# First keys and queries loaded by halves of the heads on 128 partitions, transposed 128 rows at a time

## The chip, the core and the metric

The kernel runs on one core of a Trainium2 chip. A core has five engines that run beside each other and meet through semaphores: TensorE (PE; its weight loads are listed apart, as PEld), VectorE (DVE), ScalarE (ACT), GpSimd (POOL) and SyncE (SP). TensorE reads from the on-chip memory SBUF and writes to the accumulation memory PSUM; VectorE and ScalarE carry results from there back into SBUF. Transfers run on 16 DMA engines. Both memories have 128 partitions. The metric is the device time of one execution in microseconds; the median of several plain runs counts, and a profile is one further execution that the hardware profiler recorded.

## What is computed

The inputs are q, k and v of shape 8 batches x 8 heads x 576 positions x 64, in float32, and two weight matrices, 512 x 2048 and 2048 x 512. Each head runs attention in a window of 32 positions to either side, and the joined heads go through a two-layer network:

```python
scores = (1 / sqrt(64)) * q @ k^T
mask   = abs(pos_i - pos_j) <= 32            # within one batch
attn   = softmax(where(mask, scores, -1e9))
x      = (attn @ v), heads side by side       # 4608 rows x 512
h      = x @ w_in                             # 4608 x 2048
out    = (h * sigmoid(1.702 * h)) @ w_out     # 4608 x 512, float32
```

## The kernel before

The 4608 rows (8 batches of 576) are cut into 36 units of 128 rows, and four units make a tile of 512 rows. For a unit the kernel forms scores of keys against queries per head, with keys on the partitions (`scores`), takes their exponential on ScalarE, multiplies the band mask in on VectorE (`band`), multiplies with the values on TensorE (`values`; a column of ones beside the values gives the sums), divides by them on VectorE (`norm`) and transposes the result (`x_T`, `x_T2`). The tile then goes through the two layers, later ones with Strassen-like sums that save products; tile 0 is done plainly (`layer1_plain`, `layer2_plain`).

The order of all instructions is written out by hand: each engine runs its own in the order in which the program names them, and a wait holds everything behind it on that engine. `run` calls `opening`, which deals with units 0 to 7, and then a steady loop over tiles.

The change lies in `opening`. There SBUF is empty, and TensorE has nothing to do until the first keys have come. What happens, in order:

- POOL issues all loads. Those from float32 inputs to the kernel's 16-bit tiles convert on the way. The order is: first part of the keys (320 rows of all 8 heads), first part of the queries (256 rows), the identity matrix that the transposes need (computed on POOL), values of units 0 to 2, the first quarter of `w_in`, the mask (computed on POOL), second parts of keys and queries (256 rows each), the rest of the mask (`cut_mask`), then further weights and values, and keys and queries of the next tile (`load_four`). From the ninth transfer on, each waits until the one eight places ahead of it has landed.
- `load_first` puts rows onto 64 partitions, j successive rows of a head (j is 5 or 4) on one partition, so that each contiguous piece read is j x 64 numbers. The first parts of keys and queries lie on partitions 0 to 63, the second parts on 64 to 127.
- `T_first` transposes: for each head and each of the j rows one TensorE instruction with 64 rows and 64 columns, into two PSUM banks of four heads each. A bank is copied to SBUF by VectorE or ScalarE, so that head 2 hp lies on partitions 0 to 63 and head 2 hp + 1 on partitions 64 to 127 of slot hp.
- `keep_busy` issues products of zeros into a PSUM bank that nobody reads. There are twenty ahead of the first transposes, six between those of keys and queries, four after them, and more later in the opening.
- `odd_v` copies halves of two value tiles into one on VectorE, so that each copy waits for the loads of two successive units. In VectorE's order the copies for units 0 and 1 stand ahead of the mask products of units 0 and 1, and those for units 2 and 3 ahead of the mask products of units 2 and 3.

All products come from one helper, line 70 of the program; the program's names tell them apart in the profile (`junk` unread, `sc` scores, `pv` values, `h` first layer, `o` second layer, `tp` transposes).

Of the kernel before, what the change touches and what calls it, by code (L numbers as in the profile page):

```python
# [16 lines left out]
BF16 = mybir.dt.bfloat16  # L17
# [9 lines left out]
class _Kernel:  # L27
# [107 lines left out]
    FIRST = {"k": ((0, 320, 5), (320, 256, 4)), "q": ((32, 256, 4), (288, 256, 4))}  # L135

    def load_first(self, c, part):
        if "first" not in self.stage:
            s = self.sb("g", [128, self.H, 9, self.D], BF16, 2, "kq1")
            self.stage["first"] = {"k": s[:, :, 0:5], "q": s[:, :, 5:9]}  # L140
        lo, n, j = self.FIRST[c][part]
        src = {"q": self.q, "k": self.k}[c]
        self.nc.gpsimd.dma_start(self.stage["first"][c][64 * part:64 * part + 64, :, 0:j],
                                 src[0, :, lo:lo + n, :].rearrange("h (p j) d -> p h j d", j=j))

    def kq_tile(self, t):

# [9 lines left out]
    def T_first(self, c, part, tags, engs):  # L157

        lo, n, j = self.FIRST[c][part]
        lo -= 32 * (c == "q")  # L160
        dst = self.kq_tile(0)["kq".index(c)][:, :, lo:lo + n]
        r = slice(64 * part, 64 * part + 64)
        src = self.stage["first"][c][r]
        for i, (tag, eng) in enumerate(zip(tags, engs)):
            tp = self.bank(tag, [128, 2, j, 64], BF16, "tp")
            for h in range(4):
                for x in range(j):
                    self.nc.tensor.transpose(tp[64 * (h % 2):64 * (h % 2) + 64, h // 2, x, :], src[:, 4 * i + h, x, :],  # L168
                                             self.ident[r, r])
            self.copy(eng, dst[:, 2 * i:2 * i + 2, :].rearrange("x h (p j) -> x h p j", j=j),  # L170
                      tp.rearrange("x h j p -> x h p j"))

    def load_four(self, c):

# [387 lines left out]
    def opening(self):  # L562
# [23 lines left out]
        self.load_four("q")  # L586
        self.load_w1(3)
        dve.tensor_copy(self.identh, self.ident)
        self.keep_busy(20, "E")
        self.T_first("k", 0, "AC", (dve, act))  # L590
        self.keep_busy(6, "E")
        self.T_first("q", 0, ("LA", "LB"), (dve, act))
        self.keep_busy(4, "E")
        for u in (5, 6):
            self.load_v(u)
        self.load_w2(0)
# [21 lines left out]
        h, n, gelus = [], [0], []  # L618
# [293 lines left out]
```

## Time and profile before

| what | us |
|---|---|
| median of 3 plain runs | 288.01 (287.84 to 289.57) |
| profiled execution, its own time | 289.7 |
| its span, first to last instruction | 288.0 |
| TensorE busy | 277.7 (96%) |
| VectorE busy | 218.3 (76%) |
| ScalarE busy | 193.9 (67%) |
| POOL busy | 126.9 (44%) |
| first key load, issue to landing | 5.0 |
| first query load, issue to landing | 5.7 |
| TensorE idle in the first 32 us, at most places | 1.3 at the start, 0.6 ahead of the first transposes, 1.4 ahead of the transposes of units 2 and 3 |

A row of a timeline has the start in us, the duration, the engine, the line of the program and the operation, what is written and read with its shape, and the count of successive instructions of this kind; in brackets stands the idle time ahead of it and what ended that. Durations of overlapping instructions are counted once. Matmuls are pipelined: a group's length over its count is the price of one, after a tail for the last one to drain.

### The profile page before, as it was taken

How to read it: one execution, taken by the hardware profiler on the slowest of the kernel's cores; microseconds unless marked ns; L12 is line 12 of the kernel's file. 1: busy time of each engine (PE TensorE's matmuls, PEld its weight loads, DVE VectorE, ACT ScalarE, POOL GpSimd, SP SyncE). 2: the span in 40 equal slices, each digit the busy share in tenths (PEclk: the TensorE clock that was granted, in tenths of full speed). 3: DMA queues.
4: the chain of work that ended last, by engine and by line, in shares of the span. 5: the costliest groups of instructions: out<-in, count | busy, mean ns of one | idle time of the engine just before them, and what ended most of it. 6: DMA issues, size and time to landing. Idle time of an engine off the chain costs nothing.

```text
span 288.0 us, 9119 instructions
## 1 busy us (share of the span) xinstructions
PE 277.7 (96%) x3770; PEld 229.8 (80%) x3770; DVE 218.3 (76%) x502; ACT 193.9 (67%) x340; POOL 126.9 (44%) x192
## 2 busy tenths in 40 slices
PE   7997999999999998999999999999999999999994
PEld 5775856777678887888888888888888888888883
DVE  0676798888877986798879887978788878946731
ACT  2437594789887668676967696689668865568410
POOL 8965457599499954467155917350210000000000
PEclk9999999999999999999999999999999999999999
DMA  8999999999999999999979999998432150301033
GB/s 94 188 193 198 184 204 153 177 99 140 184 134 153 209 132 198 93 180 146 182 106 181 142 177 100 193 116 148 95 77 64 47 112 12 81 2 73 2 110 112
DMA packets 146986, 37.37 MB, mean 130 GB/s; under 512 B 133888, under 2 KB 142592, under 8 KB 146944
## 3 DMA queue, kind: packets, MB, share of 16 engines
q0 software_dynamic: 104464, 18.42, 91.4%
q1 hardware_dynamic: 42032, 17.84, 34.8%
q8 instruction: 29, 0.48, 0.7%
q10 hardware_dynamic: 448, 0.52, 0.6%
q14 instruction: 13, 0.11, 0.1%
HBM read 36.83 MB, written 9.44 MB: 161 GB/s over the span
## 4 chain that ended last, share of the span: by engine, by line
PE 87%; DVE 4%; ACT 3%; issue 2%; DMA 2%; ACTq 0%; POOLq 0%
PE h L70 39%; PE o L70 36%; PE pv L70 3%; PE sc L70 3%; DVE x L294 2%; DMA kq<-in_k_dram 2%; PE junk L70 2%; ACT p L256 1%; PE tp L168 1%; PE tp L322 1%; ACT L256 1%; DVE p L264 1%; PE tp L189 1%; PE tp L232 1%; DVE rec L293 1%
## 5 line engine op out<-in xcount | busy, mean ns | idle before, releaser
L419 ACT ACTIVATE g<-h 128x512 f16<-128x512 f32 x128 | 72.1, 598 | 35.9 <-PE h L70 35.7
L70 PEld LDWEIGHTS <-g 128*128 128x128 f16 x576 | 54.5, 98 | 9.7
L70 PEld LDWEIGHTS <-a 128*128 128x128 f16 x512 | 49.3, 98 | 11.0 <-issue 0.8
L70 PE MATMUL h<-xs,a 128*128 128x256 f16 x384 | 57.6, 272 | 0.1
L70 PE MATMUL o<-w,g 128*128 128x256 f16 (+1 forms) x320 | 55.1, 294 | 0.0
L70 PEld LDWEIGHTS <-w 128*128 128x128 f16 x512 | 49.2, 98 | 7.3 <-issue 0.6
L70 PE MATMUL h<-xT,w 128*128 128x256 f16 x384 | 53.9, 273 | 0.6 <-issue 0.5
L199 POOL DMA_DIRECT2D ve<-in_v_dram x40 | 34.3, 863 | 44.0 <-issue 37.0
L70 PEld LDWEIGHTS <-gs 128*128 128x128 f16 x384 | 36.9, 98 | 6.2 <-issue 1.5
L256 ACT ACTIVATE p<-sc 128x512 bf16<-128x512 f32 x72 | 36.6, 619 | 3.7 <-PE sc L70 3.6
L70 PE MATMUL o<-b,gs 128*128 128x256 f16 x256 | 37.8, 273 | 1.3 <-issue 0.9
L70 PE MATMUL o<-b,g 128*128 128x256 f16 x256 | 37.3, 273 | 0.0
L432 DVE TENSOR_TENSOR h<-h,s 128x512 f32<-128x512 f32 x32 | 22.4, 698 | 18.7 <-PE h L70 18.7
L67 ACT COPY h<-h 128x512 f32<-128x512 f32 x32 | 18.7, 585 | 16.5 <-PE h L70 16.1
L131 POOL DMA_DIRECT2D kst<-in_k_dram x31 | 26.4, 855 | 6.9 <-PE tp L232 3.4
L131 POOL DMA_DIRECT2D qst<-in_q_dram x35 | 28.1, 805 | 2.8 <-DMA w<-in_moe_w_out_dram 2.7
L294 DVE TENSOR_TENSOR x<-pv,rec 128x256 f16<-128x256 f32 (+1 forms) x53 | 27.6, 520 | 1.8
L264 DVE TENSOR_TENSOR p<-p,mask 128x1024 bf16<-128x1024 bf16 x36 | 24.7, 687 | 2.6 <-ACT p L256 2.6
L438 DVE TENSOR_TENSOR h<-h,s 128x512 f32<-128x512 f32 x32 | 22.4, 700 | 4.7 <-PE h L70 4.2
L209 POOL COPY vo<-ve 64x264 int32<-64x264 int32 x28 | 13.1, 467 | 25.8 <-PE pv L70 24.7
L67 ACT COPY s<-h 128x512 f32<-128x512 f32 x32 | 19.1, 598 | 1.5 <-PE h L70 0.2
L70 PE MATMUL h<-xs,w 128*128 128x256 f16 x128 | 19.2, 273 | 0.0
(85 smaller groups left out, 367.9 us busy)
## 6 DMA issues: line engine op xcount, KB each, us to landing
out_dram<-o_sb SPq DMA_DIRECT2D x33, 256.0 KB, 3.0
ve<-in_v_dram POOLq DMA_DIRECT2D x32, 128.0 KB, 5.8
kst<-in_k_dram POOLq DMA_DIRECT2D x25, 128.0 KB, 5.9
qst<-in_q_dram POOLq DMA_DIRECT2D x21, 128.0 KB, 5.7
w<-in_moe_w_in_dram POOLq DMA_DIRECT2D x4, 512.0 KB, 8.7
w<-in_moe_w_out_dram POOLq DMA_DIRECT2D x4, 512.0 KB, 13.5
qst<-in_q_dram POOLq DMA_DIRECT2D x7, 96.0 KB, 5.1
kq<-in_q_dram POOLq DMA_DIRECT2D x2, 256.0 KB, 6.2
```

The lines of the kernel that those rows point to most:

```text
L67: (eng.copy if eng is self.nc.scalar else eng.tensor_copy)(out, in_)
L70: self.nc.tensor.matmul(out, lhsT, rhs, start=start, stop=stop, skip_group_check=True)
L131: self.nc.gpsimd.dma_start(t[off:off + n], src[b, :, s:s + n, :].rearrange("h s d -> s h d"))
L168: self.nc.tensor.transpose(tp[64 * (h % 2):64 * (h % 2) + 64, h // 2, x, :], src[:, 4 * i + h, x, :], self.ident[r, r])
L199: self.nc.gpsimd.dma_start(t[off:off + n, :, :self.D], self.v[b, :, s:s + n, :].rearrange("h s d -> s h d"))
L209: eng.tensor_copy(words(vo[64:128]), words(self.ve[u % 9][64:128]))
L256: self.nc.scalar.activation(p[:, eo].rearrange("k h s -> k (h s)"), sc[eo], AF.Exp, scale=self.scale)
L264: (eng or self.nc.vector).tensor_mul(pv, pv, msk.to_broadcast([128, 8, 2, SQ]))
L294: dve.tensor_mul(x[:, 4 * at:4 * (at + n), :].rearrange("p (b h) d -> p b h d", b=n), acc[:, :, :, :D], r.to_broadcast([128, n, 4, D]))
L419: act.activation(g[:, f, 256 * half:256 * half + 256], bank.rearrange("p (i n) -> p i n", i=2), AF.Gelu_apprx_sigmoid)
L432: dve.tensor_add(e, b, s7)
L438: dve.tensor_add(c, b, s7)
```

## The change

The first parts of keys and queries now use all 128 partitions: heads 0 to 3 lie on partitions 0 to 63, heads 4 to 7 on 64 to 127. Each of the two loads becomes two, one for each half of the heads. A transpose then takes 128 rows (the same rows of two heads, h and h + 4) and gives 64 x 128, so that there are half as many, of twice the columns. A PSUM bank holds heads 0, 1, 4, 5 or 2, 3, 6, 7, and the copy writes every second slot. The second parts are loaded and transposed as before, the keys' now on partitions 0 to 63. Three calls of unread products change: 60 of 96 columns for 20 of 256 in front, and 4 of 128 columns for 6 and for 4 of 256.

```diff
@@ -135,13 +135,21 @@
     FIRST = {"k": ((0, 320, 5), (320, 256, 4)), "q": ((32, 256, 4), (288, 256, 4))}
 
     def load_first(self, c, part):
+
+        D = self.D
         if "first" not in self.stage:
-            s = self.sb("g", [128, self.H, 9, self.D], BF16, 2, "kq1")
-            self.stage["first"] = {"k": s[:, :, 0:5], "q": s[:, :, 5:9]}
+            s = self.sb("g", [128, 68 * D], BF16, 2, "kq1")
+            self.stage["first"] = {("k", 0): s[:, 0:20 * D], ("q", 0): s[:, 20 * D:36 * D],
+                                   ("k", 1): s[0:64, 36 * D:68 * D], ("q", 1): s[64:128, 36 * D:68 * D]}
         lo, n, j = self.FIRST[c][part]
-        src = {"q": self.q, "k": self.k}[c]
-        self.nc.gpsimd.dma_start(self.stage["first"][c][64 * part:64 * part + 64, :, 0:j],
-                                 src[0, :, lo:lo + n, :].rearrange("h (p j) d -> p h j d", j=j))
+        src = {"q": self.q, "k": self.k}[c][0, :, lo:lo + n, :].rearrange("h (p j) d -> p h (j d)", j=j)
+        dst = self.stage["first"][c, part]
+        if part:
+            self.nc.gpsimd.dma_start(dst.rearrange("p (h x) -> p h x", h=8), src)
+            return
+        for g in range(2):
+            self.nc.gpsimd.dma_start(dst[64 * g:64 * g + 64].rearrange("p (h x) -> p h x", h=4),
+                                     src[:, 4 * g:4 * g + 4, :])
 
     def kq_tile(self, t):
 
@@ -159,16 +167,24 @@
         lo, n, j = self.FIRST[c][part]
         lo -= 32 * (c == "q")
         dst = self.kq_tile(0)["kq".index(c)][:, :, lo:lo + n]
-        r = slice(64 * part, 64 * part + 64)
-        src = self.stage["first"][c][r]
+        src = self.stage["first"][c, part].rearrange("p (h j d) -> p h j d", j=j, d=self.D)
+        r = slice(64, 128) if part and c == "q" else slice(0, 64)
         for i, (tag, eng) in enumerate(zip(tags, engs)):
-            tp = self.bank(tag, [128, 2, j, 64], BF16, "tp")
-            for h in range(4):
-                for x in range(j):
-                    self.nc.tensor.transpose(tp[64 * (h % 2):64 * (h % 2) + 64, h // 2, x, :], src[:, 4 * i + h, x, :],
-                                             self.ident[r, r])
-            self.copy(eng, dst[:, 2 * i:2 * i + 2, :].rearrange("x h (p j) -> x h p j", j=j),
-                      tp.rearrange("x h j p -> x h p j"))
+            if part:
+                tp = self.bank(tag, [128, 2, j, 64], BF16, "tp")
+                for h in range(4):
+                    for x in range(j):
+                        self.nc.tensor.transpose(tp[64 * (h % 2):64 * (h % 2) + 64, h // 2, x, :], src[:, 4 * i + h, x, :],
+                                                 self.ident[r, r])
+                self.copy(eng, dst[:, 2 * i:2 * i + 2, :].rearrange("x h (p j) -> x h p j", j=j),
+                          tp.rearrange("x h j p -> x h p j"))
+                continue
+            tp = self.bank(tag, [128, j, 2, 64], BF16, "tp")
+            for x in range(j):
+                for h in range(2):
+                    self.nc.tensor.transpose(tp[64 * h:64 * h + 64, x].rearrange("x g p -> x (g p)"), src[:, 2 * i + h, x, :],
+                                             self.ident)
+            self.copy(eng, dst[:, i:i + 3:2, :].rearrange("x g (p j) -> x g p j", j=j), tp.rearrange("x j g p -> x g p j"))
 
     def load_four(self, c):
 
@@ -586,11 +602,11 @@
         self.load_four("q")
         self.load_w1(3)
         dve.tensor_copy(self.identh, self.ident)
-        self.keep_busy(20, "E")
+        self.keep_busy(60, "E", 96)
         self.T_first("k", 0, "AC", (dve, act))
-        self.keep_busy(6, "E")
+        self.keep_busy(4, "E", 128)
         self.T_first("q", 0, ("LA", "LB"), (dve, act))
-        self.keep_busy(4, "E")
+        self.keep_busy(4, "E", 128)
         for u in (5, 6):
             self.load_v(u)
         self.load_w2(0)
```

## The prediction, made before the result was known

> **What bounds the kernel now.** I read the page first, then the chain of waits over the first 45 us, since the change touches nothing later, and then the engines' timelines there.
>
> ```profile
> span 288.0 us, 9119 instructions
> ...
> 120.00:200.00 80.00, 80.00 (x1100) 69.01 (x1099) 67.10 (x155) 60.27 (x105) 41.05 (x63) 1.00 1.66 151
> ...
> PE o L70 <- issue: 0.9, 1, 0.9
> ```
>
> The second line is a stretch of the table by windows (length, busy time of PE, PEld, DVE, ACT, POOL, granted clock, DMA share, GB/s): from 120 to 200 us TensorE is busy all 80.00 us. The third is the longest of TensorE's five waits between 32 us and the end; none of the five names a DMA. So time won or lost in the opening should arrive at the end.
>
> ```profile
> 1.33 4.97 DMA kq<-in_k_dram
> ...
> 6.34 1.35 PE tp L168 x40
> 7.70 1.40 PE junk L70 x6
> 9.09 1.02 PE tp L168 x32
> 10.11 0.97 PE junk L70 x4
> 11.08 1.00 PE sc L70 x32
> 12.08 2.02 PE junk L70 x10
> ```
>
> This is the chain (start, length, what): the first key load, then TensorE without a gap, and 2.37 us of that (1.40 + 0.97) are products that nobody reads. The chain names the last releaser only, so VectorE and ScalarE have to be read beside it:
>
> ```profile
> 10.21 0.59 ACT L67 COPY kq<-tp 128x512 bf16<-128x512 bf16 x1 [1.79 <-PE tp L168]
> 11.71 2.06 ACT L256 ACTIVATE p<-sc 128x512 bf16<-128x512 f32 x4 [0.91 <-PE sc L70]
> ...
> 11.55 0.58 DVE L210 COPY vo<-ve 64x264 int32<-64x264 int32 x1
> 12.90 0.69 DVE L264 TENSOR_TENSOR p<-p,mask 128x1024 bf16<-128x1024 bf16 x1 [0.77 <-ACT p L256]
> 13.81 0.69 DVE L264 TENSOR_TENSOR p<-p,mask 128x1024 bf16<-128x1024 bf16 x1 [0.22 <-ACT p L256]
> ```
>
> The second mask product ends at 14.50; the second unit's values cannot start before it, whatever the ten unread products do. What counts is therefore: scores, exponentials, mask products.
>
> **The change, part by part.** *The clock.* Equal products take two prices:
>
> ```profile
> 1.27 4.45 PE L70 MATMUL junk<-idle 128*128 128x256 bf16 x20 [1.27 <-DVE spark L567]
> ...
> 14.94 0.83 PE L70 MATMUL junk<-idle 128*128 128x256 bf16 x6
> 15.60 0.39 PE L310 MATMUL tp<-identh,x 128*128 128x128 f16 x4
> ...
> 28.88 1.11 PE L189 MATMUL tp<-ident,o_sb 128*64 128x128 bf16 x32
> ```
>
> At 14.94 six products of 256 columns take 0.83 us: less a tail of some 0.2, 0.107 each. At 1.27 twenty take 4.45: 0.213 each, twice as much, though the granted clock in the windows there reads 1.00. The ten from 12.08 still take 2.02, so the slow price held to about 14 us. The Trainium skill, "TensorE: Matmul & The Clock Gate", Part 1, says that the array runs at half rate until a free-running window of about 3.4 us has been busy; the trace agrees on the factor of two, and its granted-clock column does not show it.
>
> *Sixty products of 96 columns for twenty of 256.* By columns at the slow price: 0.213 x 96/256 = 0.080 each, 4.8 us, so from 1.27 to about 6.1, where the old ones were through at 5.7. The cover is the first key load, which lands at 6.30: nothing is paid. Each product also loads 128 columns of weights. At 15.60 load and product of 128 columns run at (0.39 - 0.22) / 3 = 0.057 apart, so at half rate the load costs at most 0.114, and sixty would take 6.8 us; below, it is hidden. I take hidden, because the 64x64 transposes at 6.34 have a load each and go at 0.03.
>
> *The first transposes.* Keys: 20 instructions of 128 rows for 40 of 64; queries 16 for 32. The form stands at 28.88: (1.11 - 0.22) / 32 = 0.028 fast, so 0.055 slow. Keys cost 20 x 0.055 + 0.22 = 1.3 (was 1.35), queries 1.1 (was 1.02 to 1.09). The streamed columns are the same (20 x 128 = 40 x 64): no gain from the array. At the fast price they would be 0.8 and 0.7. The copies keep their number and sizes, with another order of strides, which no row prices; I take 0, within 0.1 either way.
>
> *Unread products between.* 6 and 4 of 256 become 4 and 4 of 128: 1.40 and 0.97 become 0.43 each slow, 0.23 fast: 0.97 + 0.54 = 1.5 off TensorE's row. What is late next is the query load.
>
> *Loads.* Two transfers become four, all issued by POOL ahead of everything else it does:
>
> ```profile
> 1.33 0.82 POOL L143 DMA_DIRECT2D kq<-in_k_dram  x1 [0.80 <-POOLq L896]
> 2.14 0.69 POOL L143 DMA_DIRECT2D kq<-in_q_dram  x1
> ...
> 3.36 2.67 POOL L199 DMA_DIRECT2D ve<-in_v_dram  x3
> ...
> 9.83 0.56 POOL L111 MEMSET mask<- 64x32 bf16 x4
> ...
> 14.98 0.65 POOL L178 DMA_DIRECT2D o_sb<-in_q_dram  x1
> kq<-in_k_dram POOLq DMA_DIRECT2D x1, 320.0 KB, 5.0
> kq<-in_q_dram POOLq DMA_DIRECT2D x1, 256.0 KB, 5.7
> 3.00:3.50 0.50, 0.50 (x4) 0.38 (x3) 0.06 (x1) 0.00 (x0) 0.42 (x3) 1.00 0.73 42
> 4.50:5.00 0.50, 0.50 (x4) 0.38 (x3) 0.00 (x0) 0.00 (x0) 0.50 (x1) 1.00 1.35 198
> ```
>
> An issue of 32 KB takes 0.65, one of 256 KB 0.69, so two more cost about 1.3 us of POOL. The identity is then ready at 4.7 instead of 3.41, hidden by the load; the mask at 11.7 instead of 10.39; the value loads, the second parts and all weights are issued 1.3 later. Landing: the keys' second half is issued at about 2.05; if the latency of 4.97 held in full, keys land at 7.0. If the engines' rate decides (42 GB/s at 3 us, 198 at 4.5), the bytes are the same and they land at 6.3. I take 6.4, since half the bytes need less of that latency. The first transpose waits for both halves, and all of TensorE's order stands behind it. Queries: landed at 2.14 + 5.7 = 7.84; the last half goes out at 3.4, so 7.84 to 8.4 (3.4 + 4.97); I take 8.1.
>
> One rule speaks against this part: the Trainium skill, "DMA: Bandwidth & Descriptors", Rules for kernel authors, says that two transfers to disjoint partition halves serialize on the same engines and one transfer should be used. No run here shows it yet; it would leave only the issue time, and its result is the second rival.
>
> *Sum with the slow price throughout.* Keys land 6.4, transposed by 7.7, four products to 8.1, queries to 9.2. ScalarE's copy of them ends at 9.8 instead of 10.80: 1.0 gained. The exponentials go to 10.7 to 12.8. The mask product is held by the mask (11.7) and by the copies of values ahead of it in VectorE's order, which were through at 11.55 + 0.58 = 12.1 and will be by 12.1 to 12.4 (below). The second mask product ends at 13.5, so 1.0 is left.
>
> *With the clock open by 6 us.* Queries are the wait: 8.1 + 0.7 + a copy's end, 9.4: 1.4 gained. Exponentials end at 12.3; the bands end between 12.6 and 13.8.
>
> *What takes some back.* VectorE's next group:
>
> ```profile
> 19.78 0.30 DVE L209 COPY vo<-ve 64x264 int32<-64x264 int32 x1
> 20.09 0.29 DVE L210 COPY vo<-ve 64x264 int32<-64x264 int32 x1
> ...
> 21.79 0.69 DVE L264 TENSOR_TENSOR p<-p,mask 128x1024 bf16<-128x1024 bf16 x1 [0.51 <-ACT p L256]
> 22.77 0.69 DVE L264 TENSOR_TENSOR p<-p,mask 128x1024 bf16<-128x1024 bf16 x1 [0.29 <-ACT p L256]
> 11.11 2.27 POOL L199 DMA_DIRECT2D ve<-in_v_dram  x3
> DMA to landing us min/median/max: 5.1/5.2/5.2
> DMA to landing us min/median/max: 7.5/7.8/8.5
> 8.00:9.00 1.00, 1.00 (x6) 0.46 (x3) 0.03 (x1) 0.42 (x1) 0.93 (x3) 1.00 2.37 152
> 10.00:12.00 2.00, 2.00 (x57) 1.37 (x52) 1.91 (x5) 0.87 (x2) 1.91 (x6) 1.00 1.28 209
> ```
>
> The first three value loads land 5.1 to 5.2 us after their issue: the third, issued at about 5.1, at 10.2; now 10.2 to 11.5, and the copies that need it end by 12.4. The next three take 7.5 to 8.5: the fourth, issued at 11.11, lands at 19.6, when its copy at 20.09 is nearly due. The latency grows while the engines move 150 to 210 GB/s: loads queue behind bytes, so a later issue need not land later. Bounds: 0 and the whole 1.3. I take 0.2, nearer to the rows of full engines. Then the copies run from 19.8 to 20.8, and the mask products, which waited for exponentials, end at 22.3 instead of 23.46. The gain of 1.0 to 1.4 passes, trimmed to 1.1 to 1.5. All later transfers are issued when an earlier one has landed (POOL's own waits), so they keep their distance.
>
> Against the profiled execution's own time, 289.7 us (span 288.0 and 1.7 around it): 289.7 - 1.1 = 288.6 with the slow price, 289.7 - 1.5 = 288.2 with the clock open. The median of the plain runs is 288.01, their spread 287.84 to 289.57. The profiled time lies beside the highest. I read the lower two as executions in which the clock opened early: by the same rows the old kernel would then have its queries transposed by 8.5, its bands ended by 12.6 and, held by value copies at 19.65, its second bands by 21.9, 1.5 ahead of the profile, about the 1.7 seen. So the change brings the common execution little: what an open clock gave, the shorter unread products give too, and not twice. **Forecast 288.2 us**, own range 287.5 to 288.8.
>
> **The rivals.** *The profile's offset is constant.* Then 1.7 is a cost of profiling, the plain executions have the slow price, and the gain of 1.1 to 1.5 shows in full: 288.01 - 1.2 = 286.8. For it: the profile is above the median. Against: one plain run reached 289.57. Chance 0.27.
>
> *The split loads take the place of the unread products (slower).* If every transfer lands 1.3 later, the fourth value load lands at 20.9, the copies end at 22.1, the second bands at 23.5: nothing is gained on the profile, 289.6, and the common execution loses 1.5. It decides once that landing moves by more than about 0.4. For it: two more issues ahead of all loads; against: growing latencies at full engines. Chance 0.16.
>
> *Weight loads hold the front.* Sixty at 0.114 end at 8.1; the keys wait 1.7 and 1.5 is given back: about 289.9. Chance 0.04, by the 0.03 above.
>
> *The change does not do what it says:* the clock stays shut as before in every execution. That is the sum with the slow price, 288.6, inside the forecast's own range. Forecast with this, 0.49. The rest, 0.04, is for a larger gain, should full partitions speed the transfers.
>
> **How the numbers follow.** A difference of under 1% (2.9 us) is about what a measurement of this kernel cannot tell from no change. All cases lie inside it. Faster by more needs 1.4 us beyond the best case: 0.03; slower by more needs both slow rivals: 0.04; so 0.93 remains. The range takes the constant offset with 0.2 beyond it, 286.6, and most of the slower rival, 289.4.
>
> **What would show it.** In the new profile: a front of sixty that ends between 5 and 6.3; keys transposed from 6.3 to 6.6 and queries from 8 to 8.4; POOL's mask finished near 11.7; the fourth value load landing between 19.6 and 20.0; the second unit's bands ending before 13.7. An own time of the new profile near 288.4, close to its median, speaks for my reading of the offset; one 1.7 above its median for the constant. I am wrong if keys land after 7, or if value copies after 20.3 hold the bands.

## The result, and the profile after

The changed kernel takes 292.20 us (median of 4 runs, 291.54 to 292.70) against 288.59 (4 runs, 287.84 to 289.57): a ratio of 1.0109, 95% interval 1.0076 to 1.0142, some 3.1 us slower by the ratio (the two medians lie 3.6 apart). Nine further executions in a later comparison (below) gave 1.0094, 1.0063 to 1.0124. The forecast was 288.2 and its range ended at 289.4: wrong.

The profiled execution of the changed kernel took 291.54 us, 1.7 more than its span, as before. So the profiled executions can be compared: 1.8 us lie between the spans.

The head of the changed kernel's page, and then TensorE's timeline of it:

```profile
span 289.8 us, 9127 instructions
```

```profile
1.27 4.48 PE L70 MATMUL junk<-idle 128*128 128x96 bf16 x60 [1.27 <-DVE spark L583]
6.41 0.75 PE L185 MATMUL tp<-ident,kq 128*64 128x128 bf16 x20 [0.66 <-DMA kq<-in_k_dram]
7.09 0.40 PE L70 MATMUL junk<-idle 128*128 128x128 bf16 x4
7.76 0.64 PE L185 MATMUL tp<-ident,kq 128*64 128x128 bf16 x16 [0.27 <-DMA kq<-in_q_dram]
8.33 0.40 PE L70 MATMUL junk<-idle 128*128 128x128 bf16 x4
9.01 0.74 PE L70 MATMUL sc<-kq 64*64 64x64 bf16 x48 [0.29 <-DVE kq L67]
```

The front does what it was meant to do. Sixty unread products end at 5.75, the clock opens at 5.05 instead of 13.73 (by the changes of the clock that the two traces record), the transposes run at the fast price, and the scores start at 9.01 instead of 11.01. Here is VectorE's timeline of the same kernel:

```profile
11.18 1.27 DVE L280 TENSOR_TENSOR p<-p,mask 128x1024 bf16<-128x1024 bf16 x2
...
19.27 0.29 DVE L225 COPY vo<-ve 64x264 int32<-64x264 int32 x1
21.62 0.29 DVE L226 COPY vo<-ve 64x264 int32<-64x264 int32 x1 [2.05 <-DMA ve<-in_v_dram]
...
22.80 1.27 DVE L280 TENSOR_TENSOR p<-p,mask 128x1024 bf16<-128x1024 bf16 x2
```

The second unit's bands end at 11.18 + 1.27 = 12.45 instead of 14.50: 2.05 us gained. Ten us later nothing is left of it. The copy at 21.62 waits 2.05 us for the fourth value load, and the next bands end at 24.07 instead of 23.46. POOL's timeline of the changed kernel and, from its table of transfers, the fourth value load (size, and us from issue to landing) show how that load came to be late:

```profile
4.46 2.68 POOL L215 DMA_DIRECT2D ve<-in_v_dram  x3
...
12.24 2.28 POOL L215 DMA_DIRECT2D ve<-in_v_dram  x3
```

```profile
ve<-in_v_dram POOLq DMA_DIRECT2D x1, 128.0 KB, 9.4
```

POOL is 1.1 us later (4.46 for 3.36, 12.24 for 11.11). But the fourth value load takes 9.4 us instead of 8.5 and lands at 21.6 instead of 19.6: issued 1.13 later, it lands 2.0 later. The windows show slower engines. First the kernel before, then the changed one (columns as in the prediction; the last is GB/s, the one two before it the granted clock):

```profile
9.00:13.00 4.00, 4.00 (x90) 3.06 (x90) 2.42 (x6) 1.87 (x4) 3.91 (x10) 1.00 1.36 200
13.00:17.00 4.00, 3.83 (x66) 2.80 (x65) 3.21 (x8) 1.41 (x4) 3.47 (x5) 1.00 1.34 200
```

```profile
9.00:13.00 4.00, 2.88 (x91) 2.30 (x91) 3.16 (x8) 2.13 (x5) 3.84 (x10) 1.00 1.29 144
13.00:17.00 4.00, 2.65 (x53) 2.14 (x52) 1.76 (x6) 1.17 (x2) 3.76 (x6) 1.00 1.30 170
...
22.11:25.53 3.42, 1.82 (x39) 1.25 (x38) 3.32 (x9) 3.39 (x6) 2.75 (x4) 1.00 1.37 200
25.53:28.94 3.41, 3.36 (x20) 2.64 (x21) 1.53 (x5) 0.66 (x2) 0.46 (x2) 0.50 1.44 196
```

Between 9 and 17 us the engines move 144 and 170 GB/s where they moved 200, with the same transfers in the queue, each issued 1.1 us later. And there is a second loss, in the last line: after a window in which TensorE was busy 1.82 of 3.42 us, the granted clock is 0.50 for 3.41 us. The chains of waits, before and then after, show its price:

```profile
25.35 0.51 PE tp L322 x6
...
28.95 1.04 PE tp L189 x32
```

```profile
25.58 1.03 PE tp L338 x8
26.61 3.82 PE h L70 x24
30.43 1.04 PE tp L205 x32
```

From the transposes of units 2 and 3 (`x_T2`) to those of the next tile (`T_four`) it is 4.85 us instead of 3.60. So the trace's account is: 0.23 late at 25.58, 1.25 from the clock, 1.48 at 30.43, and 1.8 at the end. Of the last 0.3, one wait of TensorE for VectorE near 45 us makes 0.25 (0.38 for 0.13). The kernel before is no clean measure, since its traced execution had its clock shut up to 13.73. A kernel that kept the early gain (the unread products alone, below) reached the same point 2.84 earlier:

```profile
27.59 1.04 PE tp L189 x32
```

The granted clock closes for such a window in some executions of nearly every kernel here (of the kernel before in 44 of its 133 later executions), and how often is part of the result. One closed window lowers the mean clock of an execution by 0.006; below, "closed" are those executions whose mean granted clock is 0.995 or less.

### The profile page after: what moved, and what is told of

Read it like the earlier page. It is cut to its first block, busy times and chain, and to the rows that moved or that the text cites. A ratio compares the mean times of both kernels' runs of the same rounds, so it can differ in the third digit from the quotient of the medians.

```text
span 289.8 us, 9127 instructions
## 1 busy us (share of the span) xinstructions
PE 275.8 (95%) x3772; PEld 230.0 (79%) x3772; DVE 217.5 (75%) x502; ACT 193.8 (67%) x340; POOL 127.7 (44%) x194
## 4 chain that ended last, share of the span: by engine, by line
PE 82%; DVE 5%; POOL 4%; ACT 3%; DMA 3%; issue 2%; ACTq 0%; POOLq 0%
PE h L70 38%; PE o L70 36%; DMA ve<-in_v_dram 3%; PE pv L70 3%; PE sc L70 3%; DVE x L310 2%; ACT p L272 1%; DVE p L280 1%; PE tp L338 1%; POOL ve L215 1%; POOL kq L151 1%; ACT L272 1%; PE tp L205 1%; PE tp L248 1%; DVE vo L226 1%
## 5 line engine op out<-in xcount | busy, mean ns | idle before, releaser
L70 PEld LDWEIGHTS <-w 128*128 128x128 f16 x512 | 49.8, 99 | 8.1 <-issue 0.5
L70 PE MATMUL h<-xT,w 128*128 128x256 f16 x384 | 55.2, 277 | 0.8 <-DMA w<-in_moe_w_in_dram 0.4
L448 DVE TENSOR_TENSOR h<-h,s 128x512 f32<-128x512 f32 x32 | 22.3, 698 | 18.7 <-PE h L70 18.7
```

The source lines that it names most:

```text
L70: self.nc.tensor.matmul(out, lhsT, rhs, start=start, stop=stop, skip_group_check=True)
L448: dve.tensor_add(e, b, s7)
```

## The experiments

Two theories stood at the start. **L**: the loads, with two more issues ahead of everything on POOL, cost the time. **U**: the new counts of unread products cost it, through the clock. Unless said otherwise nothing of the computation is changed in these kernels; fills of POOL go to a tile that nobody reads.

### The loads alone, and the unread products alone

```diff
 # loads_alone, from the changed kernel
-        self.keep_busy(60, "E", 96)
+        self.keep_busy(20, "E")
...
-        self.keep_busy(4, "E", 128)
+        self.keep_busy(6, "E")
...
-        self.keep_busy(4, "E", 128)
+        self.keep_busy(4, "E")
 # unread_alone, from the kernel before: the same three lines the other way
```

> The split loads and the 128-row transposes, with the old unread products (20, 6 and 4 of 256 columns). Theory L (late loads: two more issues push every later load back, the second key part and the fourth value load land late, TensorE waits and then loses its clock): second key part lands near 16, fourth value load near 21, second pair of mask products ends near 24; 1 to 3.5 us slower than before. Theory U (the fewer unread columns leave TensorE idle, and that alone closes the clock): as before within 1 us, no stretch at half clock between 20 and 30 us.

> The old loads and transposes, with the new unread products (60 of 96, 4 and 4 of 128 columns). Theory L: the loads land as before (second key part 14.7, fourth value load 19.6), scores of units 0 and 1 begin near 9.2, second pair of mask products ends near 22; between 1.5 us faster and 0.5 slower than before. Theory U: half clock in a window of 3.4 us near 25 and 2 to 3.5 us slower.

Measured: the loads alone 290.69 us, ratio 1.0042 (1.0003 to 1.0081), fourth value load at 22.07, 157 GB/s between 9 and 13 us. The unread products alone 289.05, ratio 1.0003 (0.9970 to 1.0036), landing at 19.95. VectorE's timeline of the latter, and a window of it:

```profile
19.97 0.46 DVE L210 COPY vo<-ve 64x264 int32<-64x264 int32 x1 [1.89 <-DMA ve<-in_v_dram]
```

```profile
9.00:13.00 4.00, 2.64 (x90) 2.09 (x82) 2.97 (x8) 2.08 (x5) 3.91 (x10) 1.00 1.37 194
```

U falls as a cause by itself. L stands for the late landing, but the loads alone cost 1.2 us by the ratio, well under the 3.1 of the changed kernel (the two intervals just touch), and their two executions with an open clock took 287.88 and 288.73, about what the kernel before takes. The unread products win nothing either: their executions with an open clock have a median of 287.6 and those with a closed one of 289.65, and 6 of 10 were closed.

### Fill that keeps the clock open

```diff
 # from the changed kernel
+        self.keep_busy(8, "E")
         self.T_first("k", 1, "AC", (dve, dve))
...
+        self.keep_busy(6, "t")
         self.values(2, "t")
...
+        self.keep_busy(5, "t")
         self.x_T2(2, "A", dve)
```

> The changed kernel with unread products in three places where TensorE stood idle: 8 of 256 columns ahead of the second key transposes, 6 ahead of the values of unit 2 and 5 ahead of the transposes of units 2 and 3. If the closed clock is a cost of its own: no stretch at half clock between 20 and 32 us, and 1.2 to 1.7 us less than the changed kernel (some 290.6), with loads as late as there. If the closed clock only stands in for other waits: the time of the changed kernel, 292.

Measured: 290.74, ratio 1.0044 (1.0019 to 1.0070), closed in 3 of 10. The fourth value load still lands late, at 22.33, but the chain of waits of this kernel has no half-clock stretch:

```profile
26.48 0.34 PE tp L338 x6
...
27.14 2.69 PE h L70 x24
29.83 1.08 PE tp L205 x32
```

It is 3.35 us for the changed kernel's 4.85. So the closed clock is a cost of its own, 1.5 us in the traces (1.4 to 1.9 by the ratios), and the late loads remain.

### Second parts issued ahead of the mask

```diff
 # from the changed kernel
-        self.setup_mask()
         self.load_first("k", 1)
         self.load_first("q", 1)
+        self.setup_mask()
```

> The changed kernel with the second parts of keys and queries issued ahead of the mask's construction on POOL, at 7.9 and 8.6 instead of 9.56 and 10.26; the second quarter of the first weights and the fourth value load are issued when they were. Theory L with the issue as the price: second key part lands near 14.4, TensorE does not wait for it, the fourth value load still lands at 21 or later, 0 to 0.7 us faster than the changed kernel. If the engines were short of queued bytes (rate below 150 GB/s from 9 to 14 us) the rate there rises to 180 or more, the fourth value load lands near 20, and 1.5 to 3 us come back.

Measured: 291.00, ratio 1.0084 (1.0048 to 1.0120). The keys' second part, issued at 7.84 instead of 9.56, landed at 16.55 instead of 16.07: 8.7 us under way. The engines moved 167 GB/s between 9 and 13 us, and the fourth value load landed at 21.27. To have more bytes queued early brought next to nothing forward.

### The split on the same rows, and no split but the same lateness

```diff
 # split_same_rows: before, with the new unread counts
+        for h in ((slice(0, 8),) if part else (slice(0, 4), slice(4, 8))):
+            self.nc.gpsimd.dma_start(dst[:, h], src[0, h, lo:lo + n, :]...)
 # pool_delay: before, with the new unread counts
         self.load_first("q", 0)
+        for _ in range(3):
+            pool.memset(self.idle2, 1.0)
         make_identity(nc, self.ident)
```

> The old loads and 64-row transposes with the new unread products, but each of the two first loads issued as two, four heads each, all on partitions 0 to 63: the two more issues without the partition halves. Theory S (two more issues alone push and disturb everything behind them): the first weights take 7.5 us or more, the fourth value load lands at 21 to 22.5, 290 to 292 us. Theory H (the halves on partitions 64 to 127 are what slows the engines): the rate from 9 to 13 us stays near 195 GB/s, the fourth value load lands at 19.8 to 20.4, 288.5 to 289.5 us.

> The old loads and transposes with the new unread products, and three idle fills of 128x256 on POOL after the first two issues (3 x 0.36 = 1.1 us): all later issues as late as in the changed kernel, with no more transfers. Theory D (lateness alone): second key part near 16, fourth value load near 21.5, rate 125 to 165 GB/s from 9 to 13 us, 290.5 to 292 us. Against it (something about the split transfers): rate near 195, fourth value load by 20.5, within 1 us of the kernel with the unread products alone (289.05).

Measured: the split on partitions 0 to 63 gives 290.74, ratio 1.0048 (1.0012 to 1.0084), landing at 21.28, 154 GB/s. The fills, with the old two transfers, give 291.05, ratio 1.0060 (1.0034 to 1.0086). The latter's timelines of POOL and VectorE, its transfers and its windows, one behind the other:

```profile
2.81 1.08 POOL L574 MEMSET idle<- 128x256 bf16 x3
4.34 2.67 POOL L200 DMA_DIRECT2D ve<-in_v_dram  x3
12.09 2.27 POOL L200 DMA_DIRECT2D ve<-in_v_dram  x3
```

```profile
21.63 0.30 DVE L211 COPY vo<-ve 64x264 int32<-64x264 int32 x1 [1.68 <-DMA ve<-in_v_dram]
```

```profile
ve<-in_v_dram POOLq DMA_DIRECT2D x1, 128.0 KB, 9.5
```

```profile
9.00:13.00 4.00, 1.72 (x55) 1.31 (x43) 1.75 (x5) 2.06 (x4) 3.84 (x11) 1.00 1.26 146
22.28:25.70 3.42, 1.45 (x39) 0.93 (x37) 3.32 (x9) 3.39 (x6) 2.54 (x4) 1.00 1.38 200
```

Everything the changed kernel shows in the opening is there without one more transfer: the late issue, 146 GB/s, the fourth value load at 21.6, the idle window ahead of the half clock. Neither partition halves nor the number of transfers is needed; the 1.1 us of POOL ahead of the value loads are enough for that, at a smaller loss (1.0060 for 1.0109). The Trainium skill, "DMA: Bandwidth & Descriptors", Rules for kernel authors, says that transfers to disjoint partition halves serialize and that one should be used. The runs agree that the halves bring no speed, and add that a split on the same rows is no better.

### How much lateness, and where

```diff
 # third_delay:  range(1) for range(3), same place
 # delay_behind_values: the three fills behind the third value load
             self.load_v(u)
+        for _ in range(3):
+            pool.memset(self.idle2, 1.0)
         self.load_w1(0)
 # delay_behind_weights: behind load_w1(0)
 # delay_behind_parts:   behind cut_mask, ahead of load_w1(1)
```

> The kernel of the POOL delay with one fill of 0.36 us instead of three. If lateness is paid in proportion: a third of what three fills cost over the kernel with the unread products alone, 0.4 to 0.8 us, the fourth value load at 20.3 to 20.7. If there is a point from which the engines fall out of step: landings within 0.4 us of the kernel without a fill (fourth value load by 20.3), rate near 195 GB/s from 9 to 13 us, and no cost beyond 0.3 us.

> The old loads and the new unread products, with the three POOL fills (1.1 us) behind the first three value loads and ahead of the first weights. If the value loads have to be late for the engines to fall out of step: value loads in step (third landed by 10.3), rate near 195 GB/s from 9 to 15 us but for a gap at 8 to 9, fourth value load by 20.4, within 0.5 us of the kernel with the unread products alone. If it is the weights or what comes behind them: 135 to 165 GB/s there, fourth value load at 21 or later, 1 to 2 us slower.

> The same fills behind the first weights, ahead of the mask: only the second parts and what follows are late, behind a pause in the issues of 2.8 instead of 1.7 us. If the engines run dry in that pause: second key part at 15.6 or later, fourth value load at 20.8 or later, a dip of the rate between 11 and 13 us alone, 0.5 to 1.5 us slower. If the early transfers decide: fourth value load by 20.3 and no cost.

> The same three fills of POOL (1.1 us), but behind the second parts of keys and queries, ahead of the second quarter of the first weights: the fourth value load is issued as late as in the changed kernel, all earlier loads as before. By the prediction's premise (where bytes are queued, a later issue does not land later): fourth value load within 0.4 us of 19.9, time as with the unread products alone. If every late issue is paid: fourth value load at 21 or later, 1 us or more slower.

| fills | first value load issued | GB/s, 9 to 13 us | fourth value load lands | us | ratio (interval) |
|---|---|---|---|---|---|
| three, ahead of the value loads | 4.34 | 146 | 21.61 | 291.05 | 1.0060 (1.0034 to 1.0086) |
| one, ahead of them | 3.60 | 179 | 20.08 | 288.42 | 1.0003 (0.9976 to 1.0029) |
| three, behind the third | 3.35 | 182 | 20.80 | 288.18 | 0.9981 (0.9948 to 1.0013) |
| three, behind the first weights | 3.35 | 198 | 19.50 | 288.14 | 0.9991 (0.9957 to 1.0025) |
| three, behind the second parts | 3.34 | 199 | 19.67 | 289.28 | 1.0008 (0.9975 to 1.0040) |

The rates and landings are each from one traced execution, and that of the third row, at 290.14, lay above its kernel's median. The last kernel's timelines of POOL and VectorE, and its transfers:

```profile
12.33 2.27 POOL L200 DMA_DIRECT2D ve<-in_v_dram  x3
```

```profile
19.70 0.43 DVE L211 COPY vo<-ve 64x264 int32<-64x264 int32 x1 [1.55 <-DMA ve<-in_v_dram]
```

```profile
ve<-in_v_dram POOLq DMA_DIRECT2D x1, 128.0 KB, 7.3
```

The same fills placed anywhere behind the first three value loads cost nothing measurable, though the fourth value load is issued about as late as in the changed kernel (12.06 to 12.33, and 12.24). In the last kernel it takes 7.3 us and lands where it always did, so a late issue need not be a late landing. Directly behind the third value load (third row) it does land later, at 20.80 with a rate of 182 GB/s, and still without a measurable cost: a landing near 21 is not by itself the price.

### The first weights ahead of the value loads

```diff
 # from the changed kernel
+        self.load_w1(0)
         for u in (0, 1, 2):
             self.load_v(u)
-        self.load_w1(0)
```

> The changed kernel with the first quarter of the first weights issued ahead of the first three value loads. If its engines were short of queued bytes between the queries and the weights (a value load moves 128 KB per issue of 0.89 us): the rate from 5 to 15 us is 180 to 200 GB/s, the second key part lands by 15.2 and the fourth value load by 20.3 although issued at 12.2; the first bands end 1 to 2 us later, and 0.5 to 2 us come back of the changed kernel's loss. If the rate falls for another reason: 125 to 170 GB/s again, fourth value load at 21.5, and no gain.

Measured: 294.22 (4 runs), ratio 1.0204 (1.0152 to 1.0256), first value load issued at 5.22, and only 131 and 113 GB/s between 5 and 9 us. Had the engines merely been short of bytes, 512 KB earlier would have helped. The rate stayed low, so this explanation falls. (The further loss is the value loads' own: the third one's copy on VectorE starts only at 16.42.)

### Other rows for the queries, and attempts at a better kernel

```diff
 # queries_other_rows: before, with the new unread counts, first queries on 64-127, second on 0-63
+        at = 64 * (part ^ (c == "q"))
 # other_rows_filled: that, with
-        self.keep_busy(10, "E")
+        self.keep_busy(16, "E")
...
+        self.keep_busy(8, "t")
         self.values(2, "t")
 # values_ahead_filled: new unread counts, load_v(3), load_v(4) ahead of load_w1(1), 16, 12 and 5 unread products where TensorE waits
```

> The old number of loads, each whole, with the new unread products; the first queries on partitions 64 to 127 and their second part on 0 to 63 (keys as before). Theory H: the transfers to partitions 64 to 127 ahead of the weights slow the engines: 125 to 165 GB/s from 9 to 13 us, the fourth value load at 21 or later, 290.5 or more. Theories S and D: as with the unread products alone, the fourth value load near 19.9, 288 to 289.5 us.

> The kernel with whole loads, the first queries on partitions 64 to 127 and the new unread products, once more. If its place below both kernels was the transfers': ratio to the kernel before of 0.991 to 0.997 again. If it was the share of executions in which the clock closed: 0.997 to 1.002.

> A version meant to beat both: whole loads with the first queries on partitions 64 to 127, the new unread products, and 16 for 10 unread products ahead of the values of unit 0 and 8 more ahead of those of unit 2, in time in which TensorE waits. If the closed clock makes the slow executions (289.0 to 289.3 at a clock of 0.991 to 0.994, against 286.8 to 287.5 at 0.999 or more without the fill), these become rarer: 286.7 to 287.3. If it is not the clock: 287.3 or more, with the same share of executions at 289.

> A version meant to beat both: the old loads and the new unread products, the fourth and fifth value loads issued ahead of the second quarter of the first weights, and 16 for 10, 12 and 5 more unread products where TensorE waits (ahead of the values of units 0 and 2 and of the transposes of units 2 and 3). If late value loads hold the second mask products, these end near 20.5 to 21.5 instead of 22.5; if closed clocks make the slow executions of the kernel with the unread products alone (its clock was 0.991 to 0.994 in 7 of 10), they become rare: 286.5 to 288 us.

Measured: other rows first gave 287.29, ratio 0.9941 (0.9903 to 0.9978), closed in 4 of 10, and again, the same kernel, 288.61, ratio 0.9987 (0.9954 to 1.0021), closed in 6 of 10. The gain did not repeat, so it can't be put down to the transfers. With unread products that kept the clock open in all 10 it took 288.31, ratio 0.9980 (0.9952 to 1.0008). Its executions still ran from 286.83 to 289.57, so the closed clock is not the only thing by which executions of one kernel differ: in the traced one, of 289.03, TensorE waited 1.00 us at 139.5 for VectorE, which waited for a transfer. (The last expectation above counts 7 closed executions of the unread products alone; by the mark of 0.995 they are 6.) The values ahead of the second weights brought the landing of the fourth value load to 17.6 us, but then TensorE waited elsewhere, as its timeline shows:

```profile
20.44 1.92 PE L70 MATMUL h<-xT,w 128*128 128x256 f16 x16 [1.80 <-DMA w<-in_moe_w_in_dram]
```

289.59, ratio 1.0032 (1.0003 to 1.0060). None of these kernels beats the kernel before in a way that repeated.

### The changed kernel again, with one split only, and with the identity later

```diff
 # keys_split_only: the changed kernel, first queries whole on partitions 0 to 63
-        if part:
+        if part or c == "q":
 # identity_behind_values: the changed kernel
-        make_identity(nc, self.ident)
-        for u in (0, 1, 2):
+        for u in (0, 1):
             self.load_v(u)
+        make_identity(nc, self.ident)
+        self.load_v(2)
```

> The changed kernel itself, on the same chip and beside the same runs of the kernel before as the two that follow, in more executions than its first four. If its unread products, its full partitions or its new transposes cost something of their own beside the late value loads, it stays near 1.0109, above the 1.0048 to 1.0060 of the kernels whose value loads were made late in other ways (the split on the same rows, the three fills). If the late value loads with the clock are all of it, it comes to 1.004 to 1.008, with the clock closed for a stretch in most executions.

> The changed kernel with only the keys' first part split by heads on 128 partitions; the queries' first part is one load on partitions 0 to 63 again and transposed by 64 rows. One more issue than before in place of two, so the first value load is issued near 3.9 us, between the single fill (3.60, no cost) and the three fills (4.34, 1.0060). If what costs is how late the value loads are issued, the transfers between 9 and 13 us move 155 to 185 GB/s and the ratio lies at 1.000 to 1.004; if a split load costs by itself, whatever its lateness, it lies with the split on the same rows at 1.005.

> The changed kernel with the identity built behind the first two value loads: these are issued near 3.9 and 4.8 us in place of 4.46 and 5.36, the third and all later ones as in the changed kernel; the identity is ready near 6.3, just ahead of the keys. If the first value load's lateness decides, most of the loss goes and the ratio is 1.000 to 1.004; if the third one's or the first weights' does, it stays with the changed kernel.

Measured, on one chip: the changed kernel 292.05, ratio 1.0094 (1.0063 to 1.0124); the keys' split alone 288.88, ratio 1.0000 (0.9974 to 1.0026); the identity behind two value loads 291.55, ratio 1.0078 (1.0041 to 1.0114). First the keys' split alone: timelines of POOL and VectorE, and a window:

```profile
3.94 2.67 POOL L215 DMA_DIRECT2D ve<-in_v_dram  x3
```

```profile
21.04 0.29 DVE L226 COPY vo<-ve 64x264 int32<-64x264 int32 x1 [2.33 <-DMA ve<-in_v_dram]
```

```profile
9.00:13.00 4.00, 2.74 (x91) 2.19 (x90) 3.47 (x9) 2.56 (x5) 3.91 (x10) 1.00 1.41 176
```

Then the identity behind two value loads, the same views:

```profile
3.91 1.81 POOL L215 DMA_DIRECT2D ve<-in_v_dram  x2
6.25 0.90 POOL L215 DMA_DIRECT2D ve<-in_v_dram  x1
```

```profile
20.22 0.29 DVE L226 COPY vo<-ve 64x264 int32<-64x264 int32 x1 [1.61 <-DMA ve<-in_v_dram]
```

```profile
9.00:13.00 4.00, 2.72 (x91) 2.22 (x90) 3.06 (x9) 2.43 (x5) 3.83 (x10) 1.00 1.42 186
...
21.00:24.00 3.00, 1.56 (x39) 1.17 (x38) 2.43 (x5) 2.97 (x5) 2.21 (x4) 1.00 1.36 200
24.00:28.00 4.00, 3.26 (x21) 2.62 (x22) 2.18 (x8) 1.13 (x3) 1.70 (x3) 0.57 1.44 196
```

One split costs nothing and wins nothing, with POOL half as late. The third kernel was to get most of the loss back, if the first value load's lateness decided. It got most of its rate back (186 GB/s) and its fourth value load (20.2), and yet lost nearly as much. In its one trace, though, the loss is no longer the loads'. The second bands end at 21.39 + 1.27 = 22.66, ahead of the 23.46 of the kernel before. And the transposes of the next tile start a good 1 us ahead of those of the fills' kernel (second line), which cost less in the end:

```profile
29.45 1.04 PE tp L205 x32
```

```profile
30.49 1.04 PE tp L190 x32
```

What it lost is a closed window again and two pauses of TensorE for which the profile names no releaser (`issue`), the first ahead of the closed window, the second far behind the opening. The kernel with the keys' split alone (third line) has one in the middle of its 48 products of scores:

```profile
21.83 0.93 PE L70 MATMUL h<-xT,w 128*128 128x256 f16 x7 [1.29 <-issue]
112.73 0.24 PE L70 MATMUL sc<-qT,kT 64*64 64x128 bf16 x2 [1.00 <-issue]
```

```profile
21.09 0.26 PE L70 MATMUL sc<-kq 64*64 64x64 bf16 x6 [1.64 <-issue]
```

The traces of all kernels here have 17 such pauses of 0.15 us or more. Each ended 1.27 to 1.77 us after a transfer of 16 KB on the queue that the profile calls `instruction` had ended (the first one above: 20.52 and 21.83). So they look like waits for the program's own code; that rests on this timing alone, and no run tests it.

They also bear on why the changed kernel loses more than the kernels that were late in other ways. Up to the transposes of the next tile its two traces (30.43 and 29.93) are no later than those of the fills (30.49), the split on the same rows (30.38) and the loads alone (30.49). From there to the end they need 259.4 and 260.8 us, the others 258.0, 259.1 and 258.1; 0.87 and 1.37 us of that are such pauses. One or two traces of a kernel suggest this and do not prove it.

Sorting the executions by their clock separates the two losses:

| kernel | open: number, median | closed: number, median |
|---|---|---|
| before, same comparison | 15, 288.06 | 6, 289.85 |
| unread products alone | 4, 287.58 | 6, 289.65 |
| changed kernel, again | 2, 290.75 | 7, 292.17 |
| keys' split alone | 10, 288.79 | 2, 291.55 |
| identity behind two value loads | 1, 289.77 | 6, 291.56 |

In executions with an open clock the changed kernel loses 290.75 - 288.06 = 2.7 us; a closed window adds 1.4 to 1.8 to either kernel, and comes in 11 of the changed kernel's 13 executions for 6 of 21 before. The open figures of the last and the third row rest on one and two executions. Two variants of the changed kernel with the same late loads support the third: seven open executions with the fill that keeps the clock open have a median of 290.38, five with the second parts ahead of the mask 290.60. Two things don't fit so simply: the two open executions of the kernel with the three fills (290.60 and 291.49) were no faster than its eight closed ones (291.05), and three open ones of the kernel before, in the first row, took 289.80 to 289.97, like the traced one, whose clock opened only at 13.73 and then stayed open (289.7).

## Why the prediction was wrong

- **What bounds the opening** held: scores, exponentials, masks. So did the steps up to the second unit's bands: front at 5.75 (5 to 6.3 was given), weight loads hidden, keys at 6.41 (6.4), mask finished at 11.53 (11.7), bands at 12.45 (before 13.7). The queries were there by 7.76, a little earlier than 7.84 to 8.4. The early clock, left open between two sums, came in the trace.
- **The reading of the two plain medians** held in its main part: the difference of profile and median was no offset (1.7 around the span in both kernels), and the executions differ by the clock, though not by it alone. But the unread products alone gave 1.0003, so "not twice" was right for a reason half seen: the clock that opens early also closes again later. The step from "1.0 to 1.4" to "trimmed to 1.1 to 1.5" is a slip of 0.1 upwards, which changes nothing here.
- **The step that failed** is the landing: "loads queue behind bytes, so a later issue need not land later. Bounds: 0 and the whole 1.3. I take 0.2". It measured 2.0 for an issue 1.13 later, outside both bounds. The copies of values then held the bands, which ended at 24.07 and not at 22.3: 1.8 of the 3.3 us by which the profiled execution (291.54) missed 288.2. The rule holds where I had its rows from (fills behind the second parts: 12.33 issued, 19.67 landed). A copy at 21.62, held by its load, is also the sign of being wrong that the prediction named (value copies after 20.3). The rule does not hold for the 1.1 us of lateness ahead of the first value loads, after which the same bytes moved at 144 GB/s and not at 200. The bounds took the rate of the engines as given, and no row of the kernel before shows what lowers it.
- **The term that was missing** is the clock that closes again. It stood in neither the sum nor a rival: 1.25 us in the trace, 1.4 between the executions. The Trainium skill, "TensorE: Matmul & The Clock Gate", Part 1, which I drew on for the opening of the clock, also says that it closes after an idle free-running window. The trace agrees on the window's length (3.41 us) but not on idle: here 1.82 of 3.42 us busy were too few.
- **The rivals.** "The split loads take the place of the unread products" named the mechanism, the place (the fourth value load, the copies, the second bands) and the point (over 0.4 us), and gave it 0.16. Its price, 289.6, stopped at a landing 1.3 later and an unchanged clock. The weight loads, and the change that doesn't do what it says, did not occur.
- **What stays open**: why value loads issued 1 us later slow all transfers behind them for some 8 us. More bytes queued earlier did not mend it (second parts or first weights moved ahead), and a kernel that got rate and landing back lost its time elsewhere (identity behind two value loads). Nor is it settled why the changed kernel lost more (1.0094 to 1.0109) than the kernels that were late in other ways (1.0042 to 1.0060); their intervals overlap, and in the traces the difference arises behind the opening. What the pauses without a releaser are was not tested. The new transposes with all value loads at their old times were not tried.

## What to carry to other kernels

An issue put ahead of a queue's first loads can cost more than its own 0.65 us: here two did and one did not. Before calling it hidden, follow the transfer that is needed last among those behind it, and let its bound include a lower rate for the whole queue, not only the shift. Whoever makes an engine's early work shorter should look at the stretch where it then waits: after most windows in which TensorE was busy under 1.9 of 3.4 us, the next one ran at half the clock. And where executions of one kernel differ by 2 us, sort them by granted clock before reading a gain into a median, and follow the trace past the stretch that was changed.

## What was unexpected of the hardware

- The rate of the transfers differs with when the first value loads were issued, though the same transfers are queued: 144 to 167 GB/s between 9 and 13 us in the changed kernel and those with late value loads (4.34 us and later), 194 to 201 in the others but for four in between (176 to 186, issued at 3.35 to 3.94). The 16 engines ended the first weights between 12.24 and 14.76 us in the changed kernel, between 11.77 and 12.70 before.
- The clock's windows hold their grid: open at 5.05, closed at 25.53 (6.0 windows of 3.41 later), open at 28.94. Closed windows followed ones with 1.45 and 1.82 us of TensorE busy, here in the fills' and the changed kernel; the first window below, of the kernel before, with 2.01 busy, was followed by an open one. Busy time alone does not decide: in the kernel with the values ahead of the second weights a window of 1.63 was followed by an open one (the other two lines), in the second trace of the changed kernel one of 2.02 (14.01 to 17.42) by a closed one. Over the first twelve windows of all 20 traces, 11 of 13 open ones under 1.9 us busy were followed by a closed one, 1 of 11 between 1.9 and 2.1, and none above.

```profile
24.00:27.40 3.40, 2.01 (x20) 1.61 (x21) 2.76 (x9) 2.27 (x6) 1.54 (x2) 1.00 1.44 201
```

```profile
18.66:22.07 3.41, 1.63 (x15) 1.47 (x16) 1.77 (x4) 3.38 (x6) 2.55 (x4) 1.00 1.28 206
22.07:25.49 3.42, 2.58 (x50) 2.13 (x49) 1.20 (x4) 1.81 (x4) 0.89 (x1) 1.00 1.45 193
```

- Sixty products of 96 columns took 4.48 us, most of it at half rate, less than the 60 x 0.080 = 4.8 that their columns alone would take there: the weight load of each is hidden.
